# A load of two rows of wo is issued as three loads over partitions

## The chip, the cores and the metric

The kernel runs on one core of a Trainium2 chip. A core has a matrix engine (PE, with its weight load PEld), a vector engine (DVE), a scalar engine (ACT), a general engine (POOL) and a small one that mostly issues transfers (SP). Each runs its own list of instructions, and semaphores order them against each other. Transfers between the large memory and the core's own memory (128 partitions) are issued by an engine and carried out by 16 DMA engines. The metric is the device time of one execution in microseconds (us); less is better.

## The reference

One decoding step for two sequences, in bf16: an attention over cached keys and values (32 heads, 16,384 positions, head size 128, so 268 MB each for k and v), a small gated MLP on the same x, and a sigmoid gate that mixes them.

```python
def _A_ref(x, k_cache, v_cache, wq, wo):
    B, Sq, D = x.shape
    H, Dh = 32, 128
    q = (x @ wq).reshape(B, Sq, H, Dh).transpose(0, 2, 1, 3)
    scores = jnp.einsum("bhqd,bhkd->bhqk", q, k_cache) * (Dh ** -0.5)
    p = _softmax(scores, axis=-1)
    o = jnp.einsum("bhqk,bhkd->bhqd", p, v_cache)
    return o.transpose(0, 2, 1, 3).reshape(B, Sq, H * Dh) @ wo
...
x = A_x                                     # 2 x 1 x 1024
g = _sigmoid((x * gate_w).sum(-1, keepdims=True))
a = _A_ref(x, A_k_cache, A_v_cache, A_wq, A_wo)
b = _B_ref(x, B_w1, B_w2, B_w3, B_w4)
return g * a + (1 - g) * b
```

`_B_ref` is layer norm, two dense layers with a shift between, layer norm, and two dense layers of width 3584; it takes part in the prologue alone. The change touches the last product, `@ wo`: wo has 4096 x 1024 values, 8 MB.

## The kernel before

All memory for large inputs is one tile, `ring`, of five slots of 32 KB per partition. The prologue loads wq, w2, w3 and w4 into it and works out q, the gate and the MLP's part, which lies in two PSUM banks (`rows_ps`, `rows2_ps`) as the start of the final sum. Then 32 rounds follow, one for each pair of heads and sequence: SP issues one load for k and one for v (two slots, 64 KB per partition each); DVE transposes k in the slot (L647), PE multiplies it with q (L653), a softmax follows on DVE and ACT, and PE multiplies with v (L689). PE, DVE and ACT run two rounds as the body of a hardware loop; SP's list is written out in full.

The order of SP's list is that of `dma_q`: `pump` (in the kernel's text below) takes the next load as soon as the slots that it needs have been released in program order, and puts a wait on the semaphore of the engine that released them in front of it. The last two entries are wo: its rows 0 to 15 of each partition (of 32; a row is 1024 values, 2 KB) go to slot 2 in one load, rows 16 to 31 go to slot 3 in six loads, listed in `wo_runs[1]`:

- load 0: rows 16 to 23 (16 KB per partition), load 1: rows 24 to 27 (8 KB), load 2: rows 28 and 29 (4 KB)
- load 3: the first half of the columns of rows 30 and 31; loads 4 and 5: the second half of row 30 and of row 31 (1 KB each)

Each of these six has a semaphore of its own, `s_tail[k]` (dtl0 to dtl5), and only the first waits for the slot. `runs` makes a load of whole rows, `cols_of` one of a part of the columns; both cover all 128 partitions in one transfer. All are issued on SP's queue.

At the end, `do_aproj` brings the attention's result into the right layout (L710 to L719) and multiplies it with wo (L728): four matmuls of 256 columns for each row, 128 in all, in the order of the loads, each load's first matmul waiting for that load's semaphore. Two casts on DVE (L757) write `orow`, the first after the first half of the columns is complete (load 3), the second after load 5; four small stores bring it out.

Of the kernel before, what the change touches and what calls it, by code (L numbers as in the profile page):

```python
# [8 lines left out]
AX = mybir.AxisListType  # L9
BF16 = mybir.dt.bfloat16  # L10
F32 = mybir.dt.float32

ENGS = ("pe", "dve", "act", "pool", "sp")

# [106 lines left out]
def build_kernel(nc, A_x, A_k, A_v, A_wq, A_wo, B_w1, B_w2, B_w3, B_w4, gate_w, out, dbg=None):  # L121
    dbg = dbg or {}
    B, Sq, D = A_x.shape
    _, H, Sk, Dh = A_k.shape
# [3 lines left out]
    P = 128  # L128
# [25 lines left out]
    RS = SLOT // D  # L154
    QO = P // H
    assert QO * RO == Dh and RO == 2 * RS
    NQ = 4
    HQ = NQ // 2
    lo, hi_, full = (0, HQ), (HQ, HQ), (0, NQ)
    wo_runs = [[(0, RS, *full)],  # L160
               [(RS, RS // 2, *full), (RS + RS // 2, RS // 4, *full), (RO - RS // 4, RS // 8, *full),
                (RO - 2, 2, *lo), (RO - 2, 1, *hi_), (RO - 1, 1, *hi_)]]
    assert all(sum(n * qn for _, n, _, qn in runs) == RS * NQ for runs in wo_runs)
    DQ = D // NQ
    PR = 32 * (NQ - 1) + 2
    assert DQ <= 512

    with ExitStack() as st:
# [5 lines left out]
        ones_bf = sb("ones_bf", [P, P], BF16)  # L174
        ones_f = sb("ones_f", [P, P], F32)
        PermQ = sb("PermQ", [P, NBP, P], BF16)
        mask4 = sb("mask4", [P, 4], F32)
        rowm = sb("rowm", [P, 4, NU], F32)
        rowv = sb("rowv", [P, 1], F32)
        dsel = sb("dsel", [P, 4, HP], BF16)  # L180
        cAB = sb("cAB", [P, 2], F32)
        neg_half = sb("neg_half", [P, 2], F32)
        xg_row = sb("xg_row", [3, D], BF16)
# [53 lines left out]
        pl = _Plan(esems)  # L237
# [38 lines left out]
        for hp in range(HP):  # L276
# [7 lines left out]
                    waits=(ev_rowm,), sig=True)  # L284
# [4 lines left out]
                        waits=(e0,), sig=True)  # L289

        dma_q = []
        dma_done = {}
# [13 lines left out]
        def pump():  # L306
            while dma_q and all(i in slot_free for i in dma_q[0][2]):
                key, fns, slots = dma_q.pop(0)
                waits = sum((slot_free.pop(i) for i in slots), ())
                slot_of[key] = slots[0]  # L310
                slots_of[key] = slots
                for k, fn in enumerate(fns):
                    dsem = s_ring[slots[0]] if len(fns) == 1 else s_tail[k]
                    dma_done[key] = dma_done[key, k] = pl.dma("sp", (lambda e, fn=fn, idx=slots[0]: fn(e, idx)), dsem,
                                                              waits=waits if k == 0 else ())

        def release(key, ev, slots=None):
            for idx in slots or slots_of[key]:
                assert idx not in slot_free
                slot_free[idx] = tuple(ev) if isinstance(ev, (tuple, list)) else (ev,)  # L320
            pump()

        def arrived(key):
            assert key in dma_done, f"load {key} not yet issued in program order (would deadlock)"
            return dma_done[key]

        def runs(Wt, width, r0, rn, base=0):
            def fn(e, idx):
                src = Wt.rearrange("(p r) n -> p (r n)", p=P)[:, r0 * width:(r0 + rn) * width]
                flat = ring[:, idx:, :].rearrange("p s m -> p (s m)")  # L330
                return e.dma_start(flat[:, (r0 - base) * width:(r0 - base + rn) * width], src)  # L331
            return fn

        def cols_of(Wt, width, r0, rn, c0, cn, base):
            def fn(e, idx):
                dst = ring[:, idx, :].rearrange("p (r n) -> p r n", n=width)[:, r0 - base:r0 - base + rn, c0:c0 + cn]
                return e.dma_start(dst, Wt.rearrange("(p r) n -> p r n", p=P)[:, r0:r0 + rn, c0:c0 + cn])
            return fn

        wloads = {}  # L340
        wloads[("wq", 0)] = [runs(A_wq, HD, 0, NBD)]
        wloads[("w3", 0)] = [runs(B_w3, F, 0, NBD)]
        wloads[("w4", 0)] = [runs(B_w4, D, 0, NBF)]
        for hi in range(2):
            wloads[("wo", hi)] = [runs(A_wo, D, r0, rn, hi * RS) if qn == NQ else cols_of(A_wo, D, r0, rn, q0 * DQ, qn * DQ, hi * RS)
                                  for r0, rn, q0, qn in wo_runs[hi]]
        wloads[("w2", 0)] = [runs(B_w2, D, 0, NBD)]

        w_slots = {"wq": (0, 1), "w2": (2,), "w3": (3, 4), "w4": (0, 1)}
# [207 lines left out]
        key = ("w2", 0)  # L557
        put([row_stage(key, list(range(NBD)), 0, NBD, lambda kc: shT_bf[:, kc, :], "const", last=True), hs_columns], key)
        put([st_x1, ln_a(x1T_f[:, :, :], "x1", st2_ps, "xn2"), ln_b(st2_ps, "xn2", None)])
        key = ("w3", 0)  # L560
        put([dense_stage(key, [kl], NBD, NBF, h3_ps, lambda kc: xn_bf[:, kc, :], "xn2", "h3", F) for kl in range(NBD)], key)
        put([gelu2])
        key = ("w4", 0)
# [7 lines left out]
        for qd in range(NQ):  # L571
            ev_xr = pl.dma("act", lambda e, qd=qd: e.dma_start(xrow[32 * qd:32 * qd + 2, :], A_x[:, 0, qd * DQ:(qd + 1) * DQ]), s_xr,
                           waits=(ev_xr0,))
# [5 lines left out]
        for pi in range(2):  # L579
            queue_load(("wo", pi), wloads[("wo", pi)], ((2, 3)[pi],))  # L580
        pump()

        def xcols(row, b_n, nb):
# [4 lines left out]
        for nb in range(NBD):  # L588
            last = pl.add("pe", lambda e, nb=nb: e.transpose(tr_ps[:, nb * 4:nb * 4 + 3], xcols(xg_row, 3, nb), ident[0:3, 0:3]),
                          waits=(ev_x, ev_gw, ev_ident), sig=(nb == NBD - 1))  # L590
# [9 lines left out]
        key = ("wq", 0)  # L600
        wv = ring_w(slot_of[key], NBD, HD)
        for kc in range(NBD):
            for h in range(H):
# [3 lines left out]
                    waits=(arrived(key), ev_xT_bf) if h == 0 else (), sig=(h == H - 1))  # L607
# [4 lines left out]
        for bp in range(NBP):  # L612
            evp = pl.add("pe", lambda e, bp=bp: e.matmul(q4_ps[:, bp, :], lhsT=PermQ[:, bp, :],
                                                        rhs=q_sb[:, :, :].rearrange("p h b -> p (h b)"), start=True, stop=True),
                         waits=(ev_q, ev_const, ev_r0), sig=(bp == NBP - 1))
# [139 lines left out]
        for i, ps in enumerate((rows_ps, rows2_ps)):  # L755
            sl = slice(PH2 * i, PH2 * i + 32 * (HQ - 1) + B)
            ev_fin = pl.add("dve", lambda e, sl=sl, ps=ps: e.tensor_copy(orow[sl, :], ps[sl, 0:DQ]), waits=(ev_alast[i],), sig=True)  # L757
            for j, eng in enumerate(("sp", "act")):
                qd = HQ * i + j
                ev_out = pl.dma(eng, lambda e, qd=qd: e.dma_start(out[:, 0, qd * DQ:(qd + 1) * DQ], orow[32 * qd:32 * qd + 2, :]), s_out[j],  # L760
                                waits=(ev_fin,))
# [34 lines left out]
def bass_gated_mix__mha_block_cached__mixer_s_mlp__decode_kernel(  # L796
    nc: bass.Bass,
    A_x: bass.AP,
    A_k_cache: bass.AP,
    A_v_cache: bass.AP,  # L800
    A_wq: bass.AP,
    A_wo: bass.AP,
    B_x: bass.AP,
    B_w1: bass.AP,
    B_w2: bass.AP,
    B_w3: bass.AP,
    B_w4: bass.AP,
    gate_w: bass.AP,
    out: bass.AP,
):  # L810
    build_kernel(nc, A_x, A_k_cache, A_v_cache, A_wq, A_wo, B_w1, B_w2, B_w3, B_w4, gate_w, out)
# [28 lines left out]
```

## Time and profile before

| | us |
|---|---|
| median of 3 runs | 1324.66 (1324.58 to 1324.75) |
| the profiled execution | 1324.56 |
| its span, first to last instruction | 1323.0 |
| PE busy | 785.5 |
| DVE busy | 660.0 |

The profile page shows one execution. Its busy times say how long an engine worked, not what it was worth: an engine that waits for the transfers anyway costs nothing. What sets the time is read from the chain that ended last, which goes back from the last instruction to what released it, and from the waits. A line number is that of the kernel before; in the changed kernel the same lines stand 2 to 8 lines lower. "SPq" is an instruction that issues a transfer. Answers can be had for a window of time, in us from the start of the span; the row of DMA digits gives the mean busy share of the 16 DMA engines in 40 equal slices of the window, in tenths.

### The profile page before, as it was taken

To read this page: it belongs to the slowest core of one execution; us is meant where nothing else is said; L and a number is where in the kernel's file an instruction comes from. 1 tells how busy PE (TensorE), PEld (TensorE's weight loads), DVE (VectorE), ACT (ScalarE), POOL (GpSimd) and SP (SyncE) were. 2 spreads that over 40 slices of the span, in tenths; PEclk is the share of its full clock that TensorE was granted. 3 is DMA by queue.
4 is the path that set the end of the run, shared out by engine and by line. 5 is a ranking of instruction groups with operands and counts; after the bars stand their busy time and mean duration, and the time that the engine had idled before them with its cause. 6 is when DMAs were issued, how large, how long until landed. Compare 5 with 4: busy or idle time off the path is not lost.

```text
span 1323.0 us, 12293 instructions
## 1 busy us (share of the span) xinstructions
PE 785.5 (59%) x5235; PEld 335.6 (25%) x5235; DVE 660.0 (50%) x527; ACT 45.7 (3%) x99; POOL 23.6 (2%) x110
## 2 busy tenths in 40 slices
PE   2645567656556765655676565567565556756457
PEld 2512222222222222222222222222222222222223
DVE  0254446655444665544466554446655445665444
ACT  0000000000000000000000000000000000000000
POOL 3000000000000000000000000000000000000000
PEclk9977778776777877677787767888877778887778
DMA  9999999999999999999999999999999999999998
GB/s 413 437 430 433 430 434 436 430 436 434 430 438 434 430 438 432 430 438 432 430 438 432 430 438 432 430 438 432 430 438 432 434 436 430 434 436 430 436 434 367
DMA packets 10976, 570.59 MB, mean 431 GB/s; under 512 B 1219, under 2 KB 1747, under 8 KB 1878
## 3 DMA queue, kind: packets, MB, share of 16 engines
q1 hardware_dynamic: 10936, 570.43, 99.7%
q8 instruction: 8, 0.13, 0.0%
q10 hardware_dynamic: 30, 0.01, 0.0%
q14 instruction: 2, 0.02, 0.0%
HBM read 570.44 MB, written 0.00 MB: 431 GB/s over the span
## 4 chain that ended last, share of the span: by engine, by line
DMA 70%; PE 23%; DVE 6%; issue 0%; SPq 0%
DMA ring<-in_A_k_cache_dram 65%; PE ps L653 23%; DVE ring L647 6%; DMA ring<-in_B_w_dram 3%; DMA ring<-in_A_wo_dram 2%; PE ps L477 1%; SPq L331 0%; PE ps L728 0%; DVE orow L757 0%
## 5 line engine op out<-in xcount | busy, mean ns | idle before, releaser
L653 PE MATMUL ps<-ring,Z 128*128 128x512 bf16 x2048 | 533.4, 419 | 388.4 <-DVE ring L647 387.6
L647 DVE STREAM_TRANSPOSE ring<-ring 128x2048 f32<-128x2048 f32 x256 | 565.2, 2275 | 276.2 <-DMA ring<-in_A_k_cache_dram 276.2
L653 PEld LDWEIGHTS ps<-ring,Z 128*128 128x128 bf16 x2048 | 203.4, 104 | 705.7 <-issue 469.3
L689 PE MATMUL ps<-ring,PT_sb 128*32 128x512 bf16 x2048 | 169.9, 505 | 3.9 <-DVE recip L680 3.5
L703 DVE SCALAR_TENSOR_TENSOR OT_sb<-ps,gT,recip 128x2 f32 x32 | 7.0, 219 | 204.9 <-PE ps L700 204.9
L689 PEld LDWEIGHTS ps<-ring,PT_sb 128*32 128x32 bf16 x2048 | 67.9, 123 | 92.0 <-issue 71.3
L674 ACT ACTIVATE P_sb<-ps,negm 128x512 bf16<-128x512 f32 x32 | 22.0, 687 | 1006.3 <-DVE negm L672 1006.3
L663 DVE TENSOR_REDUCE rA<-ps 128x1 f32<-128x512 f32 x32 | 22.1, 692 | 64.2 <-PE ps L653 64.2
L678 PE MATMUL ps<-rowsum,hsel 128*128 128x1 f32 x128 | 24.3, 293 | 38.0 <-ACT P_sb L674 38.0
L676 DVE STREAM_TRANSPOSE PT_sb<-P_sb 128x512 bf16<-128x512 bf16 x32 | 22.8, 712 | 27.0 <-ACT P_sb L674 27.0
L634 POOL TENSOR_TENSOR Z<-q_f,mask 128x8 bf16<-128x8 f32 x64 | 12.3, 228 | 1207.7 <-PE ps L653 1207.7
L678 PEld LDWEIGHTS ps<-rowsum,hsel 128*128 128x128 f32 x128 | 21.5, 239 | 40.7 <-ACT P_sb L674 40.7
L665 PE MATMUL ps<-ident,rmax_bf 128*1 128x128 bf16 x32 | 6.9, 217 | 33.1 <-DVE rmax_bf L664 33.1
L698 ACT ACTIVATE acc_sb<-ps 128x512 bf16<-128x512 f32 x32 | 19.1, 597 | 200.6 <-PE ps L689 200.6
L700 PE MATMUL ps<-dsel,acc_sb 128*128 128x2 bf16 x128 | 8.1, 167 | 22.5 <-ACT acc_sb L698 22.5
L477 PE MATMUL ps<-xn_bf,ring 128*128 128x2 bf16 x224 | 14.4, 202 | 3.6 <-DMA ring<-in_B_w_dram 3.6
L604 PE MATMUL ps<-xT_bf,ring 128*128 128x2 bf16 x256 | 7.1, 165 | 14.6 <-DMA ring<-in_A_wq_dram 11.9
L477 PEld LDWEIGHTS ps<-xn_bf,ring 128*128 128x128 bf16 x224 | 14.3, 162 | 3.6 <-DMA ring<-in_B_w_dram 3.6
L700 PEld LDWEIGHTS ps<-dsel,acc_sb 128*128 128x128 bf16 x128 | 5.3, 96 | 38.3 <-ACT acc_sb L698 38.3
L665 PEld LDWEIGHTS ps<-ident,rmax_bf 128*1 128x1 bf16 x32 | 2.5, 79 | 48.9 <-DVE rmax_bf L664 48.9
L666 DVE TENSOR_REDUCE m_sb<-ps 1x2 bf16<-1x128 bf16 x32 | 8.9, 279 | 9.9 <-PE ps L665 9.9
L672 DVE TENSOR_SCALAR negm<-ps,cAB 128x1 f32<-128x1 f32 x32 | 8.9, 278 | 9.2 <-PE ps L669 9.2
(98 smaller groups left out, 88.7 us busy)
## 6 DMA issues: line engine op xcount, KB each, us to landing
ring<-in_B_w_dram SPq DMA_DIRECT2D x2, 7168.0 KB, 37.1
ring<-in_A_wo_dram SPq DMA_DIRECT2D x1, 4096.0 KB, 38.6
ring<-in_B_w_dram SPq DMA_DIRECT2D x1, 2048.0 KB, 26.5
ring<-in_A_wo_dram SPq DMA_DIRECT2D x1, 2048.0 KB, 22.8
ring<-in_A_wo_dram SPq DMA_DIRECT2D x1, 1024.0 KB, 25.0
ring<-in_A_k_cache_dram SPq DMA_DIRECT2D x32, 26.9
ring<-in_A_v_cache_dram SPq DMA_DIRECT2D x32, 29.2
ring<-in_A_wo_dram SPq DMA_DIRECT2D x1, 512.0 KB, 25.8
```

The source lines that it names most:

```text
L477: fn = lambda e, nb=nb, kl=kl: e.matmul(out_ps[:, nb, :], lhsT=cols(wv, kl, nb, nout), rhs=rhs_of(kl), start=False, stop=True, skip_group_ ...
L634: ev = pl.add("pool", lambda e, hp=hp: e.tensor_tensor(Z[:, :, ZO:ZO + P].rearrange("p t (i c) -> p t i c", c=32)[:, :, 2 * hp:2 * hp + 2, ...
L647: return pl.add("dve", lambda e: e.transpose(ap, ap), waits=(arrived(("k", n)),), sig=True)
L653: ev = pl.add("pe", lambda e, bp=bp: e.matmul(S_ps[:, 0:NCOL], lhsT=Z[:, bp, ZO - 2 * u:ZO - 2 * u + P], rhs=kv[:, :, bp // 2, :, bp % 2], ...
L663: e1 = pl.add("dve", lambda e: e.tensor_reduce(rA[:, :], S_ps[:, 0:NCOL], axis=AX.X, op=ALU.max), waits=(ev_S[n],), sig=True)
L665: e3 = pl.add("pe", lambda e: e.transpose(mt_ps, rmax_bf[:, :], ident[:, :]), waits=(e2,), sig=True)
L674: e7 = pl.add("act", lambda e: e.activation(P_sb[:, :], S_ps[:, 0:NCOL], ACT.Exp, bias=negm[:, 0:1], scale=scale, accum_out=rowsum[:, 0:1] ...
L676: e8 = pl.add("dve", lambda e: e.transpose(PT_sb[:, :], P_sb[:, :]), waits=(e7,), sig=True)
L678: e9 = pl.add("pe", lambda e, hp=hp: e.matmul(l_ps[:, hp:hp + 1], lhsT=hsel[:, hp, :], rhs=rowsum[:, 0:1], start=True, stop=True, skip_gro ...
L689: ev = pl.add("pe", lambda e, jj=jj, cg=cg: e.matmul(acc_ps[32 * cg:32 * cg + 32, 0:512], lhsT=PT_sb[:, 32 * jj:32 * jj + 32], rhs=vv[:, 4 ...
L698: e1 = pl.add("act", lambda e: e.activation(acc_sb[:, :], acc_ps[:, 0:512], ACT.Copy), waits=(ev_pv,), sig=True)
L700: e2 = pl.add("pe", lambda e, w=w: e.matmul(oT_ps, lhsT=acc_sb[:, w * P:(w + 1) * P], rhs=dsel[:, w, :], start=(w == 0), stop=(w == 3)), w ...
```

## The change

Load 2 of the second half of wo (rows 28 and 29 of every partition, 512 KB) is issued as three loads: partitions 0 to 26, 27 to 31 and 32 to 127. By the words of the change these run on nine, five and sixteen DMA engines, so on 3, 1 and 6 partitions for each DMA engine that takes part, where the one load has 8 for each. All three add to the same semaphore, dtl2, and the matmuls wait for the sum.

```diff
--- before.py
+++ after.py
@@ -9,6 +9,8 @@
 AX = mybir.AxisListType
 BF16 = mybir.dt.bfloat16
 F32 = mybir.dt.float32
+
+SPLIT_RUN = 2
 
 ENGS = ("pe", "dve", "act", "pool", "sp")
 
@@ -311,8 +313,9 @@
                 slots_of[key] = slots
                 for k, fn in enumerate(fns):
                     dsem = s_ring[slots[0]] if len(fns) == 1 else s_tail[k]
-                    dma_done[key] = dma_done[key, k] = pl.dma("sp", (lambda e, fn=fn, idx=slots[0]: fn(e, idx)), dsem,
-                                                              waits=waits if k == 0 else ())
+                    for f in fn if isinstance(fn, list) else [fn]:
+                        dma_done[key] = dma_done[key, k] = pl.dma("sp", (lambda e, fn=f, idx=slots[0]: fn(e, idx)), dsem, waits=waits)
+                        waits = ()
 
         def release(key, ev, slots=None):
             for idx in slots or slots_of[key]:
@@ -324,11 +327,11 @@
             assert key in dma_done, f"load {key} not yet issued in program order (would deadlock)"
             return dma_done[key]
 
-        def runs(Wt, width, r0, rn, base=0):
+        def runs(Wt, width, r0, rn, base=0, p0=0, pn=P):
             def fn(e, idx):
-                src = Wt.rearrange("(p r) n -> p (r n)", p=P)[:, r0 * width:(r0 + rn) * width]
+                src = Wt.rearrange("(p r) n -> p (r n)", p=P)[p0:p0 + pn, r0 * width:(r0 + rn) * width]
                 flat = ring[:, idx:, :].rearrange("p s m -> p (s m)")
-                return e.dma_start(flat[:, (r0 - base) * width:(r0 - base + rn) * width], src)
+                return e.dma_start(flat[p0:p0 + pn, (r0 - base) * width:(r0 - base + rn) * width], src)
             return fn
 
         def cols_of(Wt, width, r0, rn, c0, cn, base):
@@ -344,6 +347,11 @@
         for hi in range(2):
             wloads[("wo", hi)] = [runs(A_wo, D, r0, rn, hi * RS) if qn == NQ else cols_of(A_wo, D, r0, rn, q0 * DQ, qn * DQ, hi * RS)
                                   for r0, rn, q0, qn in wo_runs[hi]]
+        r0, rn, _, qn = wo_runs[1][SPLIT_RUN]
+        assert qn == NQ
+        cuts = (27, 5, 96)
+        assert sum(cuts) == P
+        wloads[("wo", 1)][SPLIT_RUN] = [runs(A_wo, D, r0, rn, RS, sum(cuts[:i]), pn) for i, pn in enumerate(cuts)]
         wloads[("w2", 0)] = [runs(B_w2, D, 0, NBD)]
 
         w_slots = {"wq": (0, 1), "w2": (2,), "w3": (3, 4), "w4": (0, 1)}
```

SP's list before, from the last v load to the output's stores (a shape is partitions by values in each; 128x16384 is the first half of wo, the rows below it loads 0 to 5; e_pe and e_dve are the semaphores of PE and DVE):

```order
L365 DMA ring<-in_A_v_cache_dram 128x32768 [waits e_pe]
L331 DMA ring<-in_A_wo_dram 128x16384
L331 DMA ring<-in_A_wo_dram 128x8192 [waits e_pe]
L331 DMA ring<-in_A_wo_dram 128x4096
L331 DMA ring<-in_A_wo_dram 128x2048
L337 DMA ring<-in_A_wo_dram 128x2x512
L337 DMA ring<-in_A_wo_dram 128x512 x2
L760 DMA out_dram<-orow 2x256 [waits e_dve] x2
```

The same place in SP's list after the change:

```order
L373 DMA ring<-in_A_v_cache_dram 128x32768 [waits e_pe]
L334 DMA ring<-in_A_wo_dram 128x16384
L334 DMA ring<-in_A_wo_dram 128x8192 [waits e_pe]
L334 DMA ring<-in_A_wo_dram 128x4096
L334 DMA ring<-in_A_wo_dram 27x2048
L334 DMA ring<-in_A_wo_dram 5x2048
L334 DMA ring<-in_A_wo_dram 96x2048
L340 DMA ring<-in_A_wo_dram 128x2x512
L340 DMA ring<-in_A_wo_dram 128x512 x2
L768 DMA out_dram<-orow 2x256 [waits e_dve] x2
```

The load of 128x2048 has become three of 27, 5 and 96 partitions at its place; loads 3 to 5 and the two stores stand two issues further back. No wait is added, and the six loads' common wait stays on load 0.

PE's list at the matmuls of loads 1, 2 and 3, before:

```order
L728 MATMUL ps<-ring,OT_sb 2x256 [waits dtl1]
L728 MATMUL ps<-ring,OT_sb 2x256 x15
L728 MATMUL ps<-ring,OT_sb 2x256 [waits dtl2]
L728 MATMUL ps<-ring,OT_sb 2x256 x7
L728 MATMUL ps<-ring,OT_sb 2x256 [waits dtl3]
L728 MATMUL ps<-ring,OT_sb 2x256 x3
```

And after the change:

```order
L736 MATMUL ps<-ring,OT_sb 2x256 [waits dtl1]
L736 MATMUL ps<-ring,OT_sb 2x256 x15
L736 MATMUL ps<-ring,OT_sb 2x256 [waits dtl2]
L736 MATMUL ps<-ring,OT_sb 2x256 x7
L736 MATMUL ps<-ring,OT_sb 2x256 [waits dtl3]
L736 MATMUL ps<-ring,OT_sb 2x256 x3
```

PE's instructions and the places of its waits are the same; what moved is what the wait on dtl2 stands for, three loads instead of one.

## The prediction

> **What bounds the kernel now.** I read the page first, then the chain that ended last, then the last few microseconds by issue, by wait and by slice. Three lines of the page:
>
> ```profile
> span 1323.0 us, 12293 instructions
> DMA packets 10976, 570.59 MB, mean 431 GB/s; under 512 B 1219, under 2 KB 1747, under 8 KB 1878
> DMA 70%; PE 23%; DVE 6%; issue 0%; SPq 0%
> ```
>
> 70% of the chain is transfer, and 570 MB at 431 GB/s are the whole span: the 16 DMA engines stream from start to end, and the other engines have only to keep up. One engine's share is 431 / 16 = 26.9 GB/s, so a piece of 4 KB takes it about 0.15 us. The change touches one load at the very end, so the end is what counts. This is the chain from 1285 us on; its columns are start, length and what it was:
>
> ```profile
> 1293.00 0.33 SPq L331
> ...
> 1293.85 0.43 SPq L331
> 1294.28 0.06 issue
> 1294.33 25.92 DMA ring<-in_A_wo_dram
> 1320.26 0.04 issue
> 1320.30 0.38 PE ps L728 x4
> 1320.68 0.01 issue
> 1320.69 0.56 PE ps L728 x4
> 1321.25 0.02 issue
> 1321.28 0.43 DVE orow L757
> ```
>
> SP issues the last six loads of wo in 3 us, and then 25.9 us pass until the fourth of them is there. That is queueing, not latency. The issue rows from 1290 us to the end, for the six loads in order (the last row is two loads), show it by size and time from issue to landing:
>
> ```profile
> ring<-in_A_wo_dram SPq DMA_DIRECT2D x1, 2048.0 KB, 22.8
> ring<-in_A_wo_dram SPq DMA_DIRECT2D x1, 1024.0 KB, 25.0
> ring<-in_A_wo_dram SPq DMA_DIRECT2D x1, 512.0 KB, 25.8
> ring<-in_A_wo_dram SPq DMA_DIRECT2D x1, 256.0 KB, 25.9
> ring<-in_A_wo_dram SPq DMA_DIRECT2D x2, 128.0 KB, 25.7
> ```
>
> Loads of 512 and of 128 KB wait the same time, each behind its predecessor. The changed load is the one of 512 KB: 32 KB for each DMA engine, eight pieces of 4 KB. PE takes the loads one after the other as they land (start, length, and in brackets the idle time before):
>
> ```profile
> 1319.65 0.10 PEld L728 LDWEIGHTS ps<-ring,OT_sb 128*2 128x2 bf16 x8 [0.30 <-DMA ring<-in_A_wo_dram]
> 1320.30 0.09 PEld L728 LDWEIGHTS ps<-ring,OT_sb 128*2 128x2 bf16 x4 [0.55 <-DMA ring<-in_A_wo_dram]
> ...
> 1320.68 0.08 PEld L728 LDWEIGHTS ps<-ring,OT_sb 128*2 128x2 bf16 x2 [0.30 <-DMA ring<-in_A_wo_dram]
> ...
> 1320.96 0.08 PEld L728 LDWEIGHTS ps<-ring,OT_sb 128*2 128x2 bf16 x2 [0.19 <-DMA ring<-in_A_wo_dram]
> ```
>
> Each of the last four loads is waited for, and the last at 1320.96. So if the DMA engine that finishes last finishes earlier, the kernel ends earlier by the same; the matmuls between two loads leave 0.2 to 0.55 us of slack.
>
> Do the 16 engines finish together? Two lines answer, each with 40 slices of a window, a digit being the mean busy share of the 16. The first is 1318.3 to 1321.1 us (slices of 70 ns), the second 1319 to 1321 us (50 ns):
>
> ```profile
> DMA  9997999869567656565764563431110000000000
> DMA  5576855655846647564544431111000000000000
> ```
>
> No. Until about 1319.0 all are busy; then the share falls to 0.5 to 0.6 and stays there until about 1319.9, falls to 0.4, and from 1320.2 to 1320.4 it is 0.1. So about **seven engines have nothing left from 1319.0 on, nine work on for a microsecond, and the last two of these for 0.2 us longer**. A load is there only when its slowest engine has written, so the seven wait for the nine. Where may the lag come from? Every load gives all 16 engines the same bytes, but instruction transfers don't. This row is from the first 150 us, the next from 1318.3 to 1321.1 us; the page has eight in all, of 0.13 MB, so 16 KB each:
>
> ```profile
> q8 instruction: 7, 0.11, 0.3%
> q8 instruction: 1, 0.02, 2.5%
> ```
>
> 16 KB cost the engine that carries them 16 / 26.9, about 0.6 us or more. In a stream that never pauses such a lag stays to the end, so up to seven engines carry one from the start. The eighth transfer falls into the tail.
>
> **The change part by part.** *Pieces.* The third load's 128 partitions come as 27, 5 and 96. Nine engines take 3 pieces each, five take 1, sixteen take 6. No view says which engines these are; in any case an engine has 6 pieces at least and 10 at most, against 8 before. Two pieces are 2 x 0.152 = 0.30 us. The end moves by between -0.30 us (those that finish last have 6) and +0.30 us (one of those has 10). If the five lie within the nine, five engines have 10, four have 9 and seven have 6. I take the lower side: seven engines are relieved, and up to seven were delayed by an instruction transfer; an engine that carried none has time to spare, about a microsecond. Of the 0.30 us I take 0.25: from 1320.2 us on only two engines are busy, so if these two are relieved, the end can come back by 0.25 us before it meets the others, should those not be relieved. **Term: -0.25 us, bounds -0.30 and +0.30.**
>
> [...] No row here shows engine numbers, so the sum goes by the bounds.
>
> *Two more issues on SP.* Each of SP's issues in the chain takes 0.43 us, with 0.04 to the next, so the third to the last part and the three loads behind go out up to 2 x 0.47 = 0.94 us later. What hides it: these loads land 25 us after their issue, since the queues are full until 1319.0. What stands behind them on SP is the output's store, and there is room:
>
> ```profile
> SPq L760 <- DVE orow L757: 25.6, 2, 25.4
> ```
>
> That is from 1290 us on: SP waits 25.4 us for the first cast. Without this cover it would be 0.94 us; term 0.
>
> *Completions.* Three parts end with 9 + 5 + 16 = 30 completion writes instead of 16; the fullest engines have two more. At the rate above a few bytes are nothing; the upper bound is a 1 KB packet each, 0.08 us. I take 0.
>
> *The wait.* The three parts count on one semaphore and PE waits for the sum, at the place where it waited before. No wait is added, and PE, DVE and ACT have the same instructions in the same order. The guard on the ring slot moves to the first part and stays in front of all six loads. Term 0, no loss possible.
>
> *Small parts.* The 5-partition part is 20 KB on five engines; its neighbours queue behind it without a gap, as the issue rows show for 128 KB loads. Term 0 below a rival's price.
>
> Sum: span 1323.0 - 0.25 = 1322.75 us. The profiled execution took 1324.56 us, 1.56 us more than its span, so 1324.31 us for one like it. The median of the runs, 1324.66 us, is 0.10 us above the profiled one: **1324.41 us**.
>
> **The rivals.**
>
> *The tail's own instruction transfer decides.* The eighth transfer costs its engine 0.6 us or more between 1318.4 and 1320. An engine that had time to spare until then becomes one of the last. If it is among those with 9 or 10 pieces, it ends 0.15 to 0.30 us later than now, and the relief of the others is not seen. It decides if that engine now ends less than 0.15 us before the last; that the share keeps at 0.1, two engines, from 1320.2 to 1320.4 allows it. About 1324.8 us.
>
> *The wrong engines.* The late ones are among those that get 9 or 10 pieces; the last then ends up to 0.30 us later: up to 1324.96 us. For it: no row names an engine. Against: seven instruction transfers, seven relieved.
>
> *It doesn't do what it says.* The parts share out so that the last engine still has its old end, or another of the nine stands right behind it: 1324.66 us. [...]
>
> *Parts slow each other.* A piece now goes to a partition that another DMA engine writes at the same time. If such pieces ran at half rate on a relieved engine, its six would cost 6 x 0.152 = 0.91 us more, less the 0.30: +0.61, 1325.27 us. It decides from two lost pieces on. No row of before shows it either way.
>
> *Parts run one after the other* (the other side). If a part on fewer engines let the next one start only after its last byte is written, two full round trips would be added. The nearest row is the output's store: the cast ends at 1321.71, the span at 1323.0, so issue and round trip take 1.29 us. Two are 2.6 us: 1324.66 + 2.58 = 1327.2 us, slower by 0.2%. It decides only if the queue drains between parts. Against it: the last loads land 0.3 to 0.65 us apart, well under a round trip.
>
> **How the numbers follow.** Chances: forecast 0.45; instruction transfer 0.22; wrong engines 0.15; no effect 0.10; parts slow each other 0.06; one after the other 0.02. The first four lie between -0.30 and +0.30 us. The three runs lie up to 0.09 us from their median, and the completions may add 0.08. So 1324.66 - 0.30 - 0.09 = 1324.27, rounded to **1324.2**, and 1324.66 + 0.30 + 0.09 + 0.08 = 1325.13, rounded to **1325.1**; outside are the last two rivals, 0.08, and the ends. A difference below 0.2%, 2.65 us, can't be told from no change by a measurement of this kernel. Only the last rival reaches it: slower 0.02, and 0.01 more for worse sharing than priced. The whole tail in which engines idle is 1.5 us, so faster by that much has no mechanism: 0.01 for what I overlooked. Within: 0.96.
>
> **What would show it.** Right: over 1318.9 to 1320.2 us the busy share is higher than 0.6 and then falls in one step; PE's waits for the last four loads start some 0.25 us earlier, the cast too; the span is 1322.7 to 1322.8 us. Instruction transfer: a share of 0.1 that lasts beyond 1320.4. Wrong engines: a lower share after 1319.0 and a later end. Slowed parts: the load of 512 KB lands after 1319.8 with every engine busy. One after the other: a gap in the slices ahead of the last loads. SP's cover: the last issue of wo some 0.9 us later, and no wait of a DMA engine from it. The prediction is wrong if the end moves by over 0.5 us, or if something away from the tail moves.

## The result and the profile after

| | before | changed |
|---|---|---|
| median | 1324.66 us (1324.49 to 1325.01) | 1326.61 us (1326.24 to 1326.94) |
| the profiled execution's span | 1323.0 us | 1325.4 us |

Both medians are of 22 runs in turn. The ratio is 1.0015, with a 95% interval of 1.0008 to 1.0021: the changed kernel is 1.95 us slower. That is under the 0.2% that the prediction took as the limit of a measurement, and outside its range (1324.2 to 1325.1 us). The two sets of runs don't overlap.

The chain that ended last in the changed kernel, from 1293.7 us on (start, length, what it was; short pieces between are left out). The four issues are load 0, load 1 and the parts of 27 and 5 partitions; the transfer is the part of 96:

```profile
1293.72 0.33 SPq L334
...
1294.09 0.43 SPq L334
...
1294.57 0.40 SPq L334
...
1295.03 0.27 SPq L334
...
1295.34 26.63 DMA ring<-in_A_wo_dram
...
1322.02 1.57 PE ps L736 x11
...
1323.62 0.43 DVE orow L765
```

Before, the chain's transfer was load 3; now it is the third part of load 2, and PE goes on at 1322.02 instead of 1319.65 us with load 2's matmuls. What the weight loads of PE waited for in the last microseconds (start, length, idle time before in brackets):

```profile
1319.74 0.52 PEld L736 LDWEIGHTS ps<-ring,OT_sb 128*2 128x2 bf16 x16 [2.45 <-DMA ring<-in_A_wo_dram]
1322.02 0.10 PEld L736 LDWEIGHTS ps<-ring,OT_sb 128*2 128x2 bf16 x8 [1.76 <-DMA ring<-in_A_wo_dram]
1322.54 0.09 PEld L736 LDWEIGHTS ps<-ring,OT_sb 128*2 128x2 bf16 x4 [0.42 <-DMA ring<-in_A_wo_dram]
1322.87 0.08 PEld L736 LDWEIGHTS ps<-ring,OT_sb 128*2 128x2 bf16 x2 [0.24 <-DMA ring<-in_A_wo_dram]
1323.20 0.08 PEld L736 LDWEIGHTS ps<-ring,OT_sb 128*2 128x2 bf16 x2 [0.24 <-DMA ring<-in_A_wo_dram]
```

The first row is load 1, which the change doesn't touch, and it is late already. The issue rows of loads 0 and 1 in the changed kernel (size, us from issue to landing):

```profile
ring<-in_A_wo_dram SPq DMA_DIRECT2D x1, 2048.0 KB, 22.1
ring<-in_A_wo_dram SPq DMA_DIRECT2D x1, 1024.0 KB, 25.6
```

Load 1 was issued at 1294.09 and so landed at 1319.7; before it was 25.0 us from 1293.37, so 1318.4. That the issues come 0.72 us later in this execution is not the reason: load 0, with the same delay, landed at 1315.8 us in both. Load 2 then is 2.4 us later than before, and the rest follows at about that distance. PE's clock is lower at the end (0.50 against 1.00 in the windows rows below), but its weight loads still wait for each transfer; from the last of these waits to the last cast it is 0.42 instead of 0.32 us.

Were the DMA engines idle or slow? The windows view of both kernels, the one of before first. Its columns are the stretch, its length, busy time and count of five engines, PE's clock, and at the end the DMA engines' busy share and the GB/s that they moved:

```profile
1314.00:1316.00 2.00, 1.57 (x32) 1.08 (x36) 0.23 (x1) 0.00 (x0) 0.00 (x0) 0.69 0.98 410
1316.00:1318.00 2.00, 2.00 (x48) 1.28 (x40) 0.00 (x0) 0.00 (x0) 0.00 (x0) 0.50 0.96 384
1318.00:1320.00 2.00, 1.99 (x64) 1.16 (x56) 0.00 (x0) 0.00 (x0) 0.00 (x0) 0.96 0.82 283
1320.00:1322.00 2.00, 0.97 (x12) 0.25 (x8) 0.84 (x2) 0.00 (x0) 0.00 (x0) 1.00 0.06 18
```

And the changed kernel:

```profile
1314.00:1316.00 2.00, 2.00 (x47) 1.24 (x39) 0.00 (x0) 0.00 (x0) 0.00 (x0) 0.50 0.95 397
1316.00:1318.00 2.00, 1.58 (x52) 1.03 (x44) 0.00 (x0) 0.00 (x0) 0.00 (x0) 0.95 1.06 290
1318.00:1320.00 2.00, 0.26 (x8) 0.20 (x12) 0.00 (x0) 0.00 (x0) 0.00 (x0) 0.91 0.98 226
1320.00:1322.00 2.00, 0.76 (x16) 0.18 (x8) 0.00 (x0) 0.00 (x0) 0.00 (x0) 0.50 0.74 185
```

To 1316 us the two are alike. Then the engines of the changed kernel are as busy as can be and move less: from 1318 to 1320 a share of 0.98 with 226 GB/s, where 0.96 had moved 384 before (from 1316 to 1318). By busy time a byte takes (0.98 / 226) / (0.96 / 384) = 1.7 times as long, though the two stretches don't hold the same mix of pieces.

The kept traces settle it piece by piece, for they have a DMA record for each piece, with its size and the time that it took. These are means over all pieces of the loads, in the profiled executions:

| | before | changed |
|---|---|---|
| load 1, pieces of 8 KB | 0.313 us | 0.366 us |
| load 2, pieces of 4 KB | 0.162 us | 0.251 us |
| loads 3 to 5, pieces of 1 KB | 0.048 us | 0.068 us |

A piece of load 2 takes 1.55 times as long. Each DMA engine has on average 8, 8 and 32 of these pieces, so the slowing adds 0.42, 0.71 and 0.62 us, together 1.75 us, to an average engine. That is most of the 1.95 us, and more than half of it falls on loads that the change leaves alone. The slices of the window 1318.3 to 1321.1 us, where before seven engines ran dry from about 1319.0 us on and all by 1320.4, are nearly full now:

```profile
DMA  9974979699949959989999989796999879779876
```

### The profile page after: what moved, and what is told of

It is laid out like the page before. It is cut to its first block, busy times and chain, and to the rows that moved or that the text cites. A ratio compares the mean times of both kernels' runs of the same rounds, so it can differ in the third digit from the quotient of the medians.

```text
span 1325.4 us, 12295 instructions
## 1 busy us (share of the span) xinstructions
PE 795.8 (60%) x5235; PEld 338.2 (26%) x5235; DVE 659.8 (50%) x527; ACT 45.7 (3%) x99; POOL 23.6 (2%) x110
## 4 chain that ended last, share of the span: by engine, by line
DMA 70%; PE 23%; DVE 6%; issue 0%; SPq 0%
DMA ring<-in_A_k_cache_dram 65%; PE ps L661 22%; DVE ring L655 6%; DMA ring<-in_B_w_dram 3%; DMA ring<-in_A_wo_dram 2%; PE ps L485 1%; SPq L334 0%; PE ps L736 0%; DVE orow L765 0%
## 5 line engine op out<-in xcount | busy, mean ns | idle before, releaser
L697 PE MATMUL ps<-ring,PT_sb 128*32 128x512 bf16 x2048 | 179.1, 527 | 4.4 <-DVE recip L688 4.1
```

Source lines behind the costliest of these rows:

```text
L697: ev = pl.add("pe", lambda e, jj=jj, cg=cg: e.matmul(acc_ps[32 * cg:32 * cg + 32, 0:512], lhsT=PT_sb[:, 32 * jj:32 * jj + 32], rhs=vv[:, 4 ...
```

## The experiments

Five explanations were held against each other: **shared writing** (parts by partitions put pieces on engines that write where another writes at the same time, and both slow down), a **price per transfer**, the **fullest engine** (10 pieces instead of 8), the **reading side**, and, for the relief, where the late engines are. All times are medians, of 11 runs (5 with load 0 cut into runs); the kernel before was measured beside each and had 1324.66 to 1324.71 us. The 95% intervals of the ratios are about 0.001 to either side, so what separates the small cases is that the same kernel's runs lie within a few tenths of a microsecond. Edits are against the changed kernel, unless told otherwise; "..." stands for lines left out.

**Three loads by columns.** `flat_cols` loads the columns from c0 on, cn of them, of all 128 partitions.

```diff
-        wloads[("wo", 1)][SPLIT_RUN] = [runs(A_wo, D, r0, rn, RS, sum(cuts[:i]), pn) for i, pn in enumerate(cuts)]
...
+        wloads[("wo", 1)][SPLIT_RUN] = [flat_cols(c0, cn) for c0, cn in ((0, D // 2), (D // 2, D // 2), (D, D))]
```

> Load 2 comes as three loads again, but cut by columns (1, 1 and 2 KB of each partition's 4 KB), each over all 128 partitions, so each DMA engine has the partitions that it has in every other load. Theory 'shared writing' (the parts by partitions put pieces on DMA engines that then write where another engine writes at the same time, and both slow down): nothing is shared, 1324.6 to 1324.9 us. Rival 'price per transfer' (two more issues, descriptors and completions on the queue cost the time): the same three transfers, so about +1.95 us, 1326.6 us. Rival 'fullest engine' (10 pieces instead of 8): balanced here, 1324.6 to 1324.7 us, but it can explain +0.3 us at most in the changed kernel.

1324.62 us (ratio 1.0, 0.9991 to 1.0009). Three transfers with their issues and completions cost nothing when each covers all partitions. The price per transfer falls.

**Cuts of 32 and 96.**

```diff
-        cuts = (27, 5, 96)
+        cuts = (32, 96)
```

> The cuts are 32 and 96 in place of 27, 5 and 96: every DMA engine has 2 + 6 = 8 pieces, balanced as in the kernel before, with one more issue than before. Theory 'shared writing': the parts still don't follow the order of full loads, +1.0 to +2.3 us, 1325.7 to 1327.0 us. 'Price per transfer': half of the change's, about +1.0 us, 1325.6 us. 'Fullest engine': balanced, 1324.6 to 1324.7 us.

1326.89 us (1.0016, 1.0007 to 1.0025), +2.23 us. If both parts are spread evenly over all sixteen engines, which the author took from the counts and no record of this run shows, every engine has eight pieces here, and neither uneven counts nor nine or five engines in place of sixteen are the cause: cutting into runs of neighbouring partitions is enough.

**The same cuts on load 0.**

```diff
-SPLIT_RUN = 2
+SPLIT_RUN = 0
```

> The same cuts 27, 5 and 96 on load 0 (rows 16 to 23, 2 MB) instead of load 2 (512 KB): the number of transfers is that of the changed kernel, the bytes are four times. 'Shared writing': the loss grows with the bytes, +4 to +8 us, 1328.5 to 1332.5 us. 'Price per transfer': 1326.6 us as in the changed kernel. 'Fullest engine': two pieces of 16 KB at 26.9 GB/s are 1.2 us, less the relief: at most 1325.9 us.

1331.34 us (1.0051, 1.0038 to 1.0065): +6.7 us for 2 MB against +1.95 us for 512 KB, 3.4 times for four times the bytes. The loss goes roughly with bytes, not with transfers.

**Another source.** Three parts with the change's cuts and destinations, read from the first 256 rows of wo.

```diff
-        wloads[("wo", 1)][SPLIT_RUN] = [runs(A_wo, D, r0, rn, RS, sum(cuts[:i]), pn) for i, pn in enumerate(cuts)]
...
+                src = A_wo[0:rn * P, :].rearrange("(p r) n -> p (r n)", p=P)[p0:p0 + pn, :]
...
+        wloads[("wo", 1)][SPLIT_RUN] = [near(sum(cuts[:i]), pn) for i, pn in enumerate(cuts)]
```

> The changed kernel with the three parts read from another place: one block of 512 KB without gaps (the first 256 rows of wo) instead of 4 KB from every 64 KB; cuts and destinations are those of the change. Rows 28 and 29 then hold other values, so this part of the product is left out. 'Shared writing': as the changed kernel, 1326.4 to 1326.9 us. Rival 'reading side' (the order in which the engines read the rows of wo from memory collides): the loss shrinks or goes, 1324.6 to 1325.6 us.

1326.36 us (1326.0 to 1326.76; ratio 1.0013, 1.0003 to 1.0022), +1.7 us, just below the expected range; its runs overlap those of the changed kernel. Most of the loss, at least, doesn't come from where the rows are read, and a 4 KB piece of load 2 took no less than in the changed kernel (0.263 us on average).

**Cuts of 64 and 64, and every second partition.** The first has `cuts = (64, 64)`; in the second the two parts are the even and the odd partitions:

```diff
+                src = A_wo.rearrange("(p t r) n -> p t (r n)", t=2, r=RO)[:, i, r0 * D:(r0 + rn) * D]
...
+                return e.dma_start(flat[i::2, (r0 - RS) * D:(r0 - RS + rn) * D], src)
```

> Cuts 64 and 64: four pieces for each DMA engine from each part, balanced, one issue fewer than in the changed kernel. [...] 'Any other order' (every piece that isn't where a full load puts it costs the same): as e2_32_96, +1.9 to +2.4 us, 1326.6 to 1327.1 us.

1326.79 us (1.0016, 1.0007 to 1.0025), +2.1 us.

> [...] 'Any other order': as e5_64_64, 1326.6 us or more.

1324.75 us (1.0001, 0.9992 to 1.001), +0.1 us. Two parts of 64 partitions each, the same pieces, bytes and transfers; one pair loses 2.1 us, the other next to nothing. What differs is which partitions are written together, and with them which rows of wo are read together; the run with another source speaks against the reading. The windows row of each from 1316 to 1318.5 us shows it, the kernel before first, then 64 and 64, then every second:

```profile
1316.00:1318.50 2.50, 2.50 (x64) 1.64 (x56) 0.00 (x0) 0.00 (x0) 0.00 (x0) 0.57 1.01 392
...
1316.00:1318.50 2.50, 1.04 (x32) 0.66 (x32) 0.00 (x0) 0.00 (x0) 0.00 (x0) 1.00 1.01 257
...
1316.00:1318.50 2.50, 1.84 (x56) 1.18 (x48) 0.00 (x0) 0.00 (x0) 0.00 (x0) 0.88 1.00 392
```

Busy all the time in each; 392, 257 and 392 GB/s. By the DMA records a 4 KB piece took 0.262 us with 64 and 64 (0.266 with 32 and 96) and 0.161 with every second, as before. 64 and 64 costs no more than 32 and 96 (+2.1 and +2.2 us), as 'any other order' has it; but by that explanation every second partition should have had 1326.6 us or more, and it had 1324.75 us.

**Every second partition on load 0.** The same with `SPLIT_RUN = 0`.

> Even and odd partitions as in e6_every_second, on load 0 (2 MB) as in e3_cut_load0, which lost 6.7 us there. [...] If cutting a load by partitions has a price by bytes whatever the order: several us, 1327 us or more.

1324.68 us (1.0, 0.9991 to 1.0009). On the load that lost 6.7 us when it was cut into runs of partitions, cutting it evenly costs nothing. The windows rows from 1310 to 1318 us, of the kernel with cuts 27, 5 and 96 on load 0 and of this one:

```profile
1310.00:1318.00 8.00, 5.85 (x101) 3.09 (x93) 0.67 (x3) 0.60 (x1) 0.00 (x0) 0.75 0.96 219
...
1310.00:1318.00 8.00, 5.91 (x122) 3.50 (x113) 0.67 (x3) 0.60 (x1) 0.00 (x0) 0.79 0.99 412
```

219 against 412 GB/s at nearly the same busy share; a 16 KB piece of load 0 took 1.12 us on average in the first and 0.61 in the second, as in the kernel before.

**Have some engines time to spare?** Three kernels made from the kernel before, each with one extra transfer behind load 1, from memory to memory and outside the ring, waited for only after the stores: 5, 16 or 9 pieces of 16 KB.

```diff
+                    if key == ("wo", 1) and k == 1:
+                        ev_extra.append(pl.dma("sp", lambda e: e.dma_start(scratch[0:5, :], A_wo.rearrange("(p r) n -> p (r n)", p=P)[0:5, 0:RS // 2 * D]), s_extra))
```

> The kernel before with one more transfer that nobody waits for until the stores are out: behind load 1, five pieces of 16 KB from memory to memory (no write into the ring), which by the words of the change run on five engines. It tests the prediction's other half, that some engines have a microsecond to spare at the end and others none. If the five are among those with time to spare: no change, 1324.5 to 1324.9 us. If they are among the late ones: 16 KB at 26.9 GB/s, +0.6 us or more, 1325.2 us or more.

1324.69 us (1.0, 0.9991 to 1.0009): nothing.

> As e7_extra_5, with sixteen pieces of 16 KB, so one on each of the sixteen engines, the late ones too: +0.6 us, 1325.2 to 1325.6 us, whatever the five of the other run do. If it doesn't change the time either, the transfer from memory to memory takes nothing from these engines and the pair tells nothing.

1325.36 us (1.0005, 0.9996 to 1.0014): +0.7 us, as one piece of 16 KB on a late engine should cost.

> [...]

1325.17 us (1.0004, 0.9995 to 1.0013): +0.5 us, where it would have been nothing if all nine engines had the time of the five. That these transfers run on five, sixteen and nine engines fits the DMA records: from 1290 us on they have 5, 16 and 9 more writes of 4 bytes than the kernel before (141, 152 and 145 packets under 512 B against 136), so one for each engine that takes part. No record names an engine; if the five are among the nine, which no run shows, then five engines can take 16 KB more and four others can't all: one of these four, at least, is late. Going from sixteen extra pieces to nine spares seven engines 16 KB each, and the end comes back by 0.19 us only (the runs of the two overlap); going on to five brings 0.48 us. The slices of the window 1319 to 1321 us show how the nine end, these of the kernel with nine extra pieces:

```profile
DMA  9799679787657864766856466553232111010000
```

From 1320.55 us on (slice 32) the share is 0.1 or nothing: a single engine or two at the very end, where in the kernel before it is nothing from 1320.4 us on.

**The relief with even writing.** Load 2 by every fourth partition and every second, so that the parts are spread over the partitions: first four parts of 27, 5, 32 and 64, then five of 27, 5, 27, 5 and 64, then three of 32, 32 and 64, then four of 25, 7, 32 and 64. Which engines a part runs on no record shows. By the author's count, an estimate, an engine has 10, 9 or 6 pieces in the first, as in the change, 12, 10 or 4 in the second and 8 in the third; it takes the five engines of a part of 5 to be among the nine of a part of 27, and parts of 32 and 64 to be spread evenly over sixteen. The fourth was meant to give most to the engines with time to spare and to relieve the others; that it does so was not shown. The parts are listed as step, first partition and number; `every` loads such a part. The edit of the first:

```diff
-        wloads[("wo", 1)][SPLIT_RUN] = [runs(A_wo, D, r0, rn, RS, sum(cuts[:i]), pn) for i, pn in enumerate(cuts)]
...
+        wloads[("wo", 1)][SPLIT_RUN] = [every(*part) for part in ((4, 3, 27), (4, 111, 5), (4, 1, 32), (2, 0, 64))]
```

> [...] If the late engines are relieved as the prediction says and writing is not shared: -0.25 us, 1324.3 to 1324.5 us. If the relief is nothing: as e6_every_second, 1324.6 to 1324.9 us. If the late ones are among those with 10 pieces, or four parts cost something: 1324.9 to 1325.3 us.

1324.98 us (1.0001, 0.9992 to 1.001), +0.3 us.

> As e9_spread_relief, with the 32 cut into 27 and 5 too: by the counts 12, 10 or 4 pieces. If the relieved engines are the late ones and the others have the microsecond to spare that e7_extra_5 showed: between -0.5 and -0.2 us, 1324.1 to 1324.5 us (less than twice the gain, since an engine that isn't relieved becomes the last). If they are not: 1325.0 us or more.

The parts are `((4, 3, 27), (4, 111, 5), (4, 1, 27), (4, 109, 5), (2, 0, 64))`: 1325.39 us (1.0005, 0.9996 to 1.0014), +0.7 us.

> The balanced partner of e9_spread_relief (1324.98 us) and e10_spread_twice (1325.39 us): every fourth partition from 3 on in one part of 32, from 1 on in one of 32, the even ones in one of 64; 2 + 2 + 4 = 8 pieces for each engine. If the losses of those two come from their uneven counts (the fullest engine is last): no loss here, 1324.6 to 1324.85 us. If they come from the finer cutting (every fourth partition shares writing again): 1324.9 to 1325.3 us.

The parts here are `((4, 3, 32), (4, 1, 32), (2, 0, 64))`: 1324.49 us (0.9999, 0.9989 to 1.0008), 0.2 us below the kernel before, with an interval that holds no change.

> [...] If relief works where it is put on engines without time to spare: -0.3 to 0 us, 1324.4 to 1324.7 us. If the end moves with the fullest engine or with the cutting all the same: 1325.0 us or more.

The parts are `((4, 3, 25), (4, 103, 7), (4, 1, 32), (2, 0, 64))`: 1325.13 us (1.0003, 0.9994 to 1.0013), +0.5 us.

Not the stepping but the uneven parts, of 27 and 5 or of 25 and 7, bring the loss. It could be the fullest engine ending last, or pieces that are slowed again. The windows rows from 1316 to 1318.5 us, of the parts 32, 32 and 64, of 27, 5, 32 and 64, and of 27, 5, 27, 5 and 64, show that the latter has a hand in it:

```profile
1316.00:1318.50 2.50, 1.03 (x36) 0.65 (x40) 0.00 (x0) 0.00 (x0) 0.00 (x0) 1.00 0.99 384
...
1316.00:1318.50 2.50, 2.50 (x68) 1.72 (x60) 0.00 (x0) 0.00 (x0) 0.00 (x0) 0.65 1.02 332
...
1316.00:1318.50 2.50, 1.04 (x32) 0.66 (x32) 0.00 (x0) 0.00 (x0) 0.00 (x0) 1.00 0.99 312
```

384, 332 and 312 GB/s at full busy share. By the DMA records a 4 KB piece took 0.162, 0.198 and 0.206 us in these three, and 0.196 in the last kernel. So the pieces of the uneven parts are slowed again, less than in runs; whether the fullest engine adds to the loss stays open. No version here is faster than the kernel before by more than its interval.

## Why the prediction was wrong

**The step that failed** is the price of a piece: "a piece of 4 KB takes it about 0.15 us", taken to hold for any engine and any partition. It was worked out from loads of 128 partitions alone, for the trace of before has no large load of another shape. In the changed kernel such a piece took 0.25 us on average instead of 0.16. With that the term for the pieces, -0.25 us with bounds of -0.30 and +0.30, has the wrong sign: it shared out pieces of one price, where the price itself went up. The prediction had this as a rival, "parts slow each other", with a chance of 0.06 and 1325.27 us. What it says of the pieces fits, they slowed; that two engines write one partition at the same time no record shows. Its chance and its price were too small. The price counted only the six pieces of a relieved engine and no other load. In fact the slowing also reaches the loads beside the parts: load 1 was 1.3 us late although it is unchanged, and the 1 KB pieces behind the parts took 1.4 times as long. A likely reason, not tested by itself, is that the engines are about 1.4 us apart (before, the early ones run dry at about 1319.0 us, the last at 1320.4), so that some write parts of load 2 while others write load 1 or loads 3 to 5.

That the loss comes from which partitions are written together is shown: not from the number of transfers (columns: none), not from the counts, if the parts of 32 and 96 are spread evenly (+2.2 us), mostly not from the place of reading (+1.7 us from another place), but gone when each part takes every second partition, for 512 KB and for 2 MB alike. Why these sets collide was not shown by itself: the records show slower pieces and fewer bytes moved (257 against 392 GB/s in the same 2.5 us, at a busy share of 1.01 and 1.00), not what a piece waits for.

**The relief of the late engines**, -0.25 us: the premise holds in one half. Five engines have 0.6 us to spare. But the argument "seven instruction transfers, seven relieved" did not give the end: with nine engines loaded the end moved by 0.5 us, so, if these are the nine of the part of 27, and the five of the part of 5 are among them, a late one is among the four that the change gave a ninth piece. No run shows that the sets lie so, nor, with it, the 10, 9 and 6 pieces; what the changed kernel's records show is the number of completions, 30 in place of 16. The prediction's first rival, that an engine of the fuller ones becomes the last, fits on the same condition; that it is the instruction transfer in the tail that makes it late was argued, not tested. That transfer also costs more than the 0.6 us that the prediction put on it as a lower bound: its own row, 2.5% of 16 engines in 2.8 us, is 1.1 us. Even without shared writing the change would then not have had its 0.25 us, since that engine took more; this is argued too, for every kernel with uneven counts also had slower pieces.

**Two more issues on SP**: right. The chain's rows give 0.40 and 0.27 us for two of the parts, and nothing came to wait for the issue itself; the column kernel, with the same number, has the time of before. The cover was needed there: its last two issues of wo held SP for 5.5 and 7.2 us, to 1309.1 us, and SP still waited 12 us for the first cast.

**Completions and the wait**: right, by the same kernel, whose median is 0.04 us from that of the kernel before. The DMA records of the changed kernel have 14 more writes of 4 bytes than before (150 packets under 512 B from 1290 us on, against 136), as 9 + 5 + 16 = 30 completions in place of 16 should bring.

**Parts run one after the other**: no. There is no gap in the slices from 1318.3 to 1321.1 us; the engines' busy share was 1.06, 0.98 and 0.74 in the three stretches from 1316 to 1322 us, at whose end load 2 landed.

**The limit of 0.2%**, below which a difference "can't be told from no change", was wider than needed: the runs of one kernel lie within 0.7 us, and medians of 22 show 1.95 us clearly.

## What to carry to other kernels

A transfer's price holds for the shape from which it was read: here bytes by rate were no price for a load over fewer partitions while others were in flight (0.16 us for 4 KB from loads of 128 partitions, 0.25 us in the change's parts), and the tell-tale was a busy share that stayed at its top while GB/s fell (0.98 with 226 GB/s, against 0.96 with 384). In this kernel a load could be cut by columns (1324.62 us), or by every second partition (1324.75 and 1324.68 us), at no cost, but not into runs of neighbouring partitions (1326.61 to 1331.34 us). Before work is moved between DMA engines to even out their ends, an extra transfer that nobody waits for, over 5, 9 or 16 engines, can tell cheaply how many of them have time to spare (here nothing, +0.5 and +0.7 us for 16 KB on each).

## What the runs showed of the hardware

Cutting 512 KB into two halves of partitions cost 2.1 us, into even and odd partitions 0.1 us, at the same bytes and pieces. For 2 MB the like cuts cost 6.7 us (runs of 27, 5 and 96) and nothing (even and odd), and the busy engines' rate was 219 against 412 GB/s. A 4 KB piece took 0.16 us in a load over all partitions or every second one, 0.25 to 0.27 us in one of the parts by runs, and the pieces of the uncut loads next to it slowed as well (8 KB: 0.31 to 0.37 us). The engines of this stream didn't end together: before, some were dry from about 1319.0 us on and the last at 1320.4 us, and an extra 16 KB on five of them was free, on nine it cost 0.5 us, on sixteen 0.7 us.
